# Local attention with a SiLU feed-forward gate on one core: four chunks of the attention output are turned by DMA on planes in the used-up tile of x, not by TensorE

## The chip, the core and the metric

The kernel runs on one core of a Trainium2 chip. The metric is the device time of one execution in microseconds (us); smaller is better. PE is TensorE (matmuls and transposes; PEld is its weight loading), DVE is VectorE, ACT is ScalarE, POOL is GpSimd, SP is SyncE, which in this kernel only issues transfers.

## The reference

Batch 1, S = 2048 tokens, D = 640, F = 1536, 32 heads of 20. All inputs and the output are float32.

```python
def _A_ref(x, wqkv, wo):                    # W, dil = 8, 2
    qkv = (x @ wqkv).reshape(B, S, 3, H, Dh).transpose(2, 0, 3, 1, 4)
    q, k, v = qkv[0], qkv[1], qkv[2]
    off = jnp.arange(W) * dil
    idx = jnp.arange(S)[:, None] - off[None, :]
    mask = idx >= 0
    ...
    logits = jnp.einsum("bhsd,bhswd->bhsw", q, kg) * Dh ** -0.5
    logits = jnp.where(mask[None, None, :, :], logits, -1e9)
    o = jnp.einsum("bhsw,bhswd->bhsd", softmax(logits), vg)
    return o.transpose(0, 2, 1, 3).reshape(B, S, D) @ wo

def _B_ref(x, w1, w2):
    return silu(x @ w1) @ w2

xn = layernorm(x)
out = x + _A_ref(xn, wqkv, wo) * silu(_B_ref(xn, w1, w2))
```

Each token looks at itself and the seven tokens 2, 4, ... 14 places before it.

## The kernel before, in words

**Tokens.** The 2048 tokens are worked in four groups, g = 0 to 3, of 512: two halves of the sequence, in each the even and the odd tokens. A group is four tiles t of 128 tokens. D = 640 is five chunks c of 128.

**Exact products.** A float32 matrix is kept as a high and a low part (fp32r), and a product is three matmuls: high by high, low by high, high by low. The turned x of a group stands in TH and TL (`th`, `tl` in rows), 128 columns of D on the partitions.

**Stages.** For each group `qkv_phase` computes q, k and v in four quarters of 160 columns (NQ = 4, CQ = 160; matmuls L960 to L962) and copies them out (ACT, L715 and L717); `halo` fetches the keys and values of neighbouring tokens (L728, L738 and L740 on SP). Attention runs on DVE with some help of POOL, quarter by quarter, and ends in the tile O (`o`; L754 and L757 are the scores, L774 is the exp, L796 to L809 the values). It lags behind PE and goes on during `ffn_phase`. There, twelve units of w1 (L1140 to L1142) and twelve of w2 (L1005, L1007) give the gate, evacuated with SiLU by ACT (L1224) into G (`gate`). Behind the first unit of w1 stands `wo_phase` of the group before, five chunks of wo, which needs the O of that group turned. `wo_last` does it for the last group.

**Turning O.** wo_phase reads O chunk by chunk with columns on the partitions, in OH and OL, which share memory with the TH and TL that the current group doesn't use. PE turns a chunk with `o_chunk`: four transposes of 128x128 into a PSUM bank `rot` (L629), a high part by ACT (L633), a low part by DVE (L639). This stands in the qkv phase of the next group, at the quarters and chunks of `O_AT`. Some chunks are turned by DMA (`turn_o`): `send` copies the chunk into two planes of 2-byte halves (ACT, L657), two DMA transposes turn them (SP, L662), and `join` puts the halves together (ACT, L670), then takes the high part (ACT, L676) and the low part (DVE, L677). `turn_x` does the same for chunks of the next group's x. The planes are borrowed memory: KV tiles for `turn_os`, the gate tile and the tile TURN for x. `O_DMA` names the chunks of O turned so: 0 and 1 of the second group (g=1), 0, 1 and 2 of the last.

**x.** XIN (`xin`) holds the x of the next group: loaded by SP (L600) at the start of ffn_phase, with statistics and normalisation on DVE (L607, L609, L615, L619) and a square root on ACT (L613), then turned. From then on it lies unused until the next load of x, or, at the end, until wo_last loads x again for the residual (L1085).

**Weights.** Seven ring slots (RING = 7, `w`). A unit is first loaded raw (SP, L538, into `xr` among others) and split by ACT (L574) and DVE (L578). Then it is either written to DRAM as both halves (`half_...`, SP, L583) or read again from there by POOL (L565) each time it is due. A transfer into a slot waits until PE has read the unit that stood there and, where that was written out, until that is done. The wo of the group g=2 is split anew and written out, with its loads at the end of that group's qkv.

**Order.** All work is first collected in a planner (`Weave`): each operation has an engine, an estimated length, the keys it reads and writes, a priority and an earliest time `at`. PE keeps the order in which the code adds its work; on the other engines the planner picks by estimated ready time and priority. What comes out is one fixed list for each engine; an engine runs its list in that order and waits where something isn't ready. `clock[0]` is the sum of PE's estimated work so far. `free_for(old, new)` hands memory from one set of names to another.

Of the kernel before, what the change touches and what calls it, by code (L numbers as in the profile page):

```python
# [8 lines left out]
F32 = mybir.dt.float32  # L9
# [6 lines left out]
P = 128  # L16
# [7 lines left out]
T = 4  # L24
# [33 lines left out]
O_OUT = (), (35.0, 55.0), (35.0, 55.0), (10.0, 25.0, 40.0)  # L58
O_BACK = (), (80.0, 82.0), (80.0, 82.0), (40.0, 55.0, 60.0)
X_BY = {1: 2, 3: 0, 4: 1}  # L60
SLOW, ISSUE, SUB_LATE = 8, 2.0, 3
PACE0, PACE = -20.0, 12.0
BACK = {1: 0.0, 2: 40.0}
QAT = 48
OAT = 16
STORE_Q = 1, 3
SHARED = (1, 0), (1, 2), (2, 0), (2, 2), (3, 0)
X_AT = 1.2, 6, 8
# [255 lines left out]
def local_attention_silu_ffn(ctx: ExitStack, tc: tile.TileContext, x, wqkv, wo, w1, w2, out):  # L324
# [152 lines left out]
    def store_at(u):  # L477

        return 1 + (u[0] == "wo" or u[0] == "q" and u[2] in STORE_Q)


    for u in units:
        n = seen[u] = seen.get(u, 0) + 1
        at = store_at(u)
        what.append("load" if n > at else "store" if n == at and n < again[u] else "split")
    fresh = [i for i, k in enumerate(what) if k != "load"]
# [13 lines left out]
    def raw_tile(k):  # L500
# [7 lines left out]
        return "xr", k % 3  # L508

    def raw_load(k):  # L510
# [12 lines left out]
        pairs = []  # L523
        if u[0] == "q":
            _, q, c = u
            whole = wqkv[c * P:(c + 1) * P, :]
            pairs.append((r.rearrange("p (k m) -> p k m", k=3), whole.rearrange("p (k m) -> p k m", k=3)[:, :, q * CQ:(q + 1) * CQ]))
        elif u[0] == "w1":
            pairs.append((r.rearrange("p (c f) -> p c f", c=DC),
                          w1.rearrange("(c p) f -> p c f", p=P)[:, :, u[1] * P:(u[1] + 1) * P]))  # L530
        else:
            m = wo if u[0] == "wo" else w2
            pairs.append((r, m[u[1] * P:(u[1] + 1) * P, :]))
        by = nc.scalar if k in BY_ACT else nc.sync

        def go():
            for to, frm in pairs:
                by.dma_start(to, frm)  # L538
# [3 lines left out]
        dma(go, [], kr, n * P * 4, 1 + k if k < 2 * DC else clock[0] + 5, (0.62 if k < 2 * DC else 0.45) * len(pairs))  # L542

    def raws_due(i, k):

        while rawn[0] < len(fresh) and fresh[rawn[0]] <= i + RAW_AHEAD and raw_in.get(raw_tile(rawn[0]), -1) <= k:
            raw_load(rawn[0])
            rawn[0] += 1

    def w_load():  # L550
# [10 lines left out]
        kh, kl = ("wh", s), ("wl", s)  # L561
        due = clock[0]
        if what[i] == "load":
            src = halves[u]
            add("POOL", 1.0, lambda: nc.gpsimd.dma_start(both, src), [("half", u)], [kh, kl], due + 10,  # L565
                nbytes=2 * n * P * 4)
            raws_due(i, sum(j < i for j in fresh) - 1)
            return
# [11 lines left out]
        if what[i] == "store":  # L580
            kept = dram.tile([P, 2, n], F32, name="half_" + "_".join(map(str, u)))
            halves[u] = kept
            dma(lambda: nc.sync.dma_start(kept, both.bitcast(F32)), [kh, kl], [("half", u)], 2 * n * P * 4, due + 25)  # L583
        raws_due(i, k)
# [60 lines left out]
    def both(k):  # L645
        return [k + (0,), k + (1,)]
# [33 lines left out]
    def turn_x(c, i, by, to, at, back):  # L680
# [3 lines left out]
             (chunk_span("x", c, True), chunk_span("x", c)))  # L684

    def turn_o(c, i, by, to, at, back):
# [494 lines left out]
    def ffn_phase(g, i, ix, io):  # L1181
# [12 lines left out]
        by_dma = X_DMA.get(g, ())  # L1194
        bufs = [("buf", c, h) for c in range(DC) for h in range(2)]
        for kind, f in plan(g):
            if kind == "w1":
                up(g, i, f, io)
            elif kind == "wo":
# [8 lines left out]
                for k, c in enumerate(by_dma):  # L1208
                    by = (piece(G, X_BY[c]), ("buf", X_BY[c])) if c in X_BY else (TURN, ("turn",))
                    turn_x(c, ix, by, (piece(G, c), ("buf", c)), clock[0] + PACE0 + PACE * k, clock[0] + BACK[g])  # L1210
            elif kind == "x":
# [13 lines left out]
        if g < NG - 1:  # L1225
            turn_os(g, i, begun)

    add("POOL", 0.7, consts, [], ["consts"], 0)
# [38 lines left out]
```

## Time and profile before

| what | value |
| --- | --- |
| median of 3 runs | 598.78 us (598.73 to 599.15) |
| profiled execution | 598.41 us |
| its span in the trace | 596.3 us |
| granted TensorE clock | 0.999 |
| busy: PE, DVE, ACT, POOL | 590.6, 513.3, 248.7, 168.2 us |

The span runs from the first to the last instruction in the trace; the 2.1 us between it and the execution's time lie around it. Busy times are of one execution. Rows in the trace give start, duration, engine, line and operation, with the idle time ahead of it and what ended it in brackets. A queue (SPq) row is an issue of a transfer, not its landing.

### The profile page before, as it was taken

The page shows a single profiled execution, that of the slowest core. Times are in us where ns is not written, and L with a number is a line of the kernel's source. Part 1 is how long each engine was busy: PE and PEld are TensorE (multiplying, and loading weights), DVE is VectorE, ACT ScalarE, POOL GpSimd, SP SyncE. Part 2 cuts the span into 40 slices and gives each one's busy share as a digit, 9 for nine tenths or more (in the row PEclk, how much of TensorE's full clock was granted, in tenths as well). Part 3 has the DMA queues.
Part 4 walks back from the last instruction along what each step waited for, and adds up shares of the span by engine and source line. Part 5 has one row for each costly group of instructions (what it writes and reads, how often), then busy time and mean ns, then how long its engine had stood idle before and what let it go on. Part 6 is the DMA issues. An engine that isn't in the chain of part 4 may idle for free.

```text
span 596.3 us, 9080 instructions
## 1 busy us (share of the span) xinstructions
PE 590.6 (99%) x3443; PEld 555.9 (93%) x3443; DVE 513.3 (86%) x505; ACT 248.7 (42%) x444; POOL 168.2 (28%) x229
## 2 busy tenths in 40 slices
PE   8999999999999999999999999999999999999997
PEld 7999999999999999999999999999999999999997
DVE  6499999999799978999988996999838799998744
ACT  5437375452545223747523604443412333335230
POOL 5800102233110153442221126543121233434100
PEclk9999999999999999999999999999999999999999
DMA  9999999879999999999699999998689999797952
GB/s 295 311 295 334 296 411 402 322 252 300 271 316 326 313 257 324 239 202 239 191 319 306 303 346 304 263 208 286 211 220 283 294 320 295 227 203 215 241 185 89
DMA packets 80263, 164.21 MB, mean 275 GB/s; under 512 B 19949, under 2 KB 44237, under 8 KB 80221
## 3 DMA queue, kind: packets, MB, share of 16 engines
q1 hardware_dynamic: 60381, 83.93, 52.1%
q0 software_dynamic: 19296, 79.31, 46.5%
q8 instruction: 27, 0.44, 0.3%
q10 hardware_dynamic: 544, 0.41, 0.2%
q14 instruction: 15, 0.12, 0.1%
HBM read 107.91 MB, written 34.16 MB: 238 GB/s over the span
## 4 chain that ended last, share of the span: by engine, by line
PE 98%; DMA 0%; DVE 0%; issue 0%
PE acc L1005 23%; PE acc L1007 15%; PE acc L960 10%; PE acc L961 10%; PE acc L962 10%; PE rot L1140 9%; PE rot L1142 9%; PE rot L1141 9%; PE acc L910 2%; PE rot L629 1%; DMA xin<-in_A_x_dram 0%; PE rot L894 0%; PE rot L1123 0%; DVE st L879 0%; PE rot L853 0%; DVE gate L1091 0%
## 5 line engine op out<-in xcount | busy, mean ns | idle before, releaser
L960 PE MATMUL acc<-w,th 128*128 128x480 f32 x300 | 110.6, 369 | 0.0
L961 PE MATMUL acc<-w,tl 128*128 128x480 f32 x300 | 109.8, 366 | 0.0
L962 PE MATMUL acc<-w,th 128*128 128x480 f32 x300 | 109.8, 366 | 0.0
L1005 PE MATMUL acc<-w,sh 128*128 128x384 f32 x384 | 108.6, 328 | 0.0
L1007 PE MATMUL acc<-w,sh 128*128 128x256 f32 x384 | 104.7, 273 | 0.0
L754 DVE TENSOR_TENSOR pr<-q,kv 128x2560 f32<-128x2560 f32 x32 | 90.2, 2819 | 15.9 <-DMA kv<-carry 12.7
L796 DVE TENSOR_TENSOR pr<-q,kv 128x2560 f32<-128x2560 f32 x32 | 91.5, 2860 | 1.4 <-DVE l L757 0.5
L1140 PE MATMUL rot<-th,w 128*128 128x512 f32 x240 | 91.8, 383 | 0.0
L1141 PE MATMUL rot<-tl,w 128*128 128x512 f32 x240 | 91.0, 379 | 0.0
L1142 PE MATMUL rot<-th,w 128*128 128x512 f32 x240 | 91.0, 379 | 0.0
L757 DVE TENSOR_REDUCE l<-pr 128x128 f32<-128x2560 f32 x32 | 89.7, 2804 | 0.2
L1153 ACT ACTIVATE sh<-rot 128x512 fp32r<-128x512 f32 x48 | 28.8, 599 | 134.2 <-PE rot L1142 134.1
L565 POOL DMA_DIRECT2D w<-half_w x72 | 39.0, 542 | 156.6 <-PE acc L1007 57.6
L1007 PEld LDWEIGHTS acc<-w,sh 128*128 128x128 f32 x384 | 73.7, 192 | 0.6
L1005 PEld LDWEIGHTS acc<-w,sh 128*128 128x128 f32 x384 | 72.6, 189 | 0.6
L565 POOL DMA_DIRECT2D w<-half_q x52 | 28.0, 538 | 119.8 <-PE acc L962 74.3
L962 PEld LDWEIGHTS acc<-w,th 128*128 128x128 f32 x300 | 56.7, 189 | 4.0
L960 PEld LDWEIGHTS acc<-w,th 128*128 128x128 f32 x300 | 56.7, 189 | 3.9
L961 PEld LDWEIGHTS acc<-w,tl 128*128 128x128 f32 x300 | 56.7, 189 | 3.9
L1005 PE MATMUL acc<-w,sl 128*128 128x384 f32 x192 | 55.9, 328 | 0.0
L1155 DVE TENSOR_TENSOR sl<-sf,sh 128x512 fp32r<-128x512 f32 x48 | 39.3, 819 | 16.8 <-ACT sf L1154 16.8
L1007 PE MATMUL acc<-w,sl 128*128 128x256 f32 x192 | 52.3, 273 | 0.0
(110 smaller groups left out, 1070.0 us busy)
## 6 DMA issues: line engine op xcount, KB each, us to landing
w<-half_w POOLq DMA_DIRECT2D x72, 640.0 KB, 7.0
w<-half_q POOLq DMA_DIRECT2D x52, 480.0 KB, 5.8
half_w<-w SPq DMA_DIRECT2D x24, 640.0 KB
half_q<-w SPq DMA_DIRECT2D x20, 480.0 KB
kv<-kv SPq DMA_DIRECT2D x15, 560.0 KB
w<-half_wo POOLq DMA_DIRECT2D x10, 640.0 KB, 5.6
kv<-kv SPq DMA_DIRECT2D x15, 420.0 KB
gate<-in_B_w_dram SPq DMA_DIRECT2D x16, 320.0 KB
```

Of the source, the lines that this page charges most:

```text
L565: add("POOL", 1.0, lambda: nc.gpsimd.dma_start(both, src), [("half", u)], [kh, kl], due + 10, nbytes=2 * n * P * 4)
L754: dve(2560, lambda: nc.vector.tensor_tensor(out=PR, in0=win(qq[:, t:t + 2, :], W, 0), in1=win(kv[:, 0, t:t + 2, :], W, CQ), op=OP.mult), h ...
L757: dve(2560, lambda: nc.vector.tensor_reduce(out=l[:, t:t + 2].rearrange("p t w h -> p (t w h)"), in_=PR.rearrange("p t w (h d) -> p (t w h ...
L796: dve(2560, lambda: nc.vector.tensor_tensor(out=PR.rearrange("p t w (h d) -> p t (w h) d", d=DH), in0=e[:, t:t + 2].rearrange("p t w h -> ...
L960: nc.tensor.matmul(o, hi, vh, start=c == 0, stop=False)
L961: nc.tensor.matmul(o, lo, vh, start=False, stop=False)
L962: nc.tensor.matmul(o, hi, vl, start=False, stop=c == DC - 1)
L1005: nc.tensor.matmul(a[t][0][:, :CA].rearrange("p (m h) -> p m h", h=2), st, col_a(w), start=first, stop=last)
L1007: nc.tensor.matmul(b[t // 2][0][:, h * CB:(h + 1) * CB].rearrange("p (m h) -> p m h", h=2), st, col_b(w), start=first and h == 0, stop=las ...
L1140: nc.tensor.matmul(to, wh[:, cs], hi, start=c == 0, stop=False)
L1141: nc.tensor.matmul(to, wh[:, cs], lo, start=False, stop=False)
L1142: nc.tensor.matmul(to, wl[:, cs], hi, start=False, stop=c == DC - 1)
```

## The change

A new table, `O_HOME`, names four more chunks of O that are turned by DMA: chunk 2 of g=1 and chunks 0, 1 and 2 of g=2. `qkv_phase` leaves them out on PE. The new `turn_home` adds them at the end of the group's own `ffn_phase`, behind `turn_os`: a chunk takes two pieces of XIN as its two planes, and the third chunk the last piece and TURN. `at` is given relative to the end of that ffn_phase, and `join` 20 us later. XIN is handed over ahead and back behind, so that the next load into it waits until the planes are read.

```diff
+O_HOME = {1: {2: 5.0}, 2: {0: -9.0, 1: -6.0, 2: -3.0}}
+HOME_BACK = 20.0
...
+    def turn_home(g, i):
+
+        todo = O_HOME.get(g, {})
+        if not todo:
+            return
+        old = [("xin", t) for t in range(T)]
+        place = [(piece(XIN, k), ("xp", k)) for k in range(DC)] + [(TURN, ("turn",))]
+        new = [k for _, p in place[:DC] for k in both(p)]
+        free_for(old, new)
+        for n, (c, at) in enumerate(todo.items()):
+            turn_o(c, i, place[2 * n], place[2 * n + 1], clock[0] + at, clock[0] + at + HOME_BACK)
+        free_for(new, old)
...
                         for k in O_AT.get((q, c), ()):
-                            if k not in O_DMA.get(g - 1, ()):
+                            if k not in O_DMA.get(g - 1, ()) and k not in O_HOME.get(g - 1, ()):
                                 o_chunk(g - 1, k, io)
...
         if g < NG - 1:
             turn_os(g, i, begun)
+            turn_home(g, i)
```

The rest of the diff adds settings that are empty or repeat the old values (`turn_first`, `STORE_W2`, `RAW_AGAIN`, `PACE0` as a table) and moves code into functions. It adds no instruction. Line numbers rise by 7 to 37: of what is spoken of here, L538 is now L545, L565 is L581, L574 is L590, L578 is L594, L583 is L577, L600 is L614, L607 is L621, L609 is L623, L619 is L633, L629 is L643, L633 is L647, L639 is L653, L657 is L671, L662 is L676, L670 is L684, L676 is L690, L677 is L691, L774 is L808, L1085 is L1119, L1153 to L1155 are L1187 to L1189, L1224 is L1261.

The lists move at three places that matter here.

SP at the end of the third group's qkv, before. `kv_96` is the last quarter's tile, `carry` the rows kept for the other half, `xr` takes raw weights (and x for the residual), `w_77` to `w_79` are ring slots with the first three chunks of wo:

```order
L738 DMA kv_96<-carry_121 1x2x640
L538 DMA xr_107<-in_A_wo_dram 128x640
L740 DMA kv_96<-carry_121 2x2x480
L538 DMA xr_108<-in_A_wo_dram 128x640
L583 DMA half_wo_167<-w_77 128x1280
L583 DMA half_wo_168<-w_78 128x1280
L583 DMA half_wo_169<-w_79 128x1280
L1053 DMA xr_109<-in_A_x_dram 128x640
```

The same place after the change, with the four loads of x around the raw loads of wo:

```order
L774 DMA kv_96<-carry_121 2x2x480
L614 DMA xin<-in_A_x_dram 128x640
L545 DMA xr_107<-in_A_wo_dram 128x640
L545 DMA xr_108<-in_A_wo_dram 128x640
L614 DMA xin<-in_A_x_dram 128x640 x3
L577 DMA half_wo_167<-w_77 128x1280
L577 DMA half_wo_168<-w_78 128x1280
L577 DMA half_wo_169<-w_79 128x1280
L1087 DMA xr_109<-in_A_x_dram 128x640
```

Before, the four loads stand some 12 rows ahead of this, behind the carry of the second quarter. Now they stand behind the carry of the last, and ahead of the stores of wo.

DVE at the start of the third group's FFN, before. L1155 is the low part of the first SiLU unit, `w_80` and `w_81` are the last two chunks of wo, which PE reads next; L780 to L783 and L796 belong to the attention:

```order
L780 TENSOR_REDUCE z_91<-q_97 128x32
L782 RECIPROCAL z_91<-z_91 128x32
L783 TENSOR_TENSOR q_97<-q_97,z_91 128x4x64
L1155 TENSOR_TENSOR sl_87<-sf,sh_84 128x512
L578 TENSOR_TENSOR w_80<-xr_107,w_80 128x640
L578 TENSOR_TENSOR w_81<-xr_108,w_81 128x640
L796 TENSOR_TENSOR pr<-q_97,kv_93 128x2560
```

The same place after:

```order
L653 TENSOR_TENSOR tl_74<-rot_120,th_70 128x512
L621 BN_STATS st_72<-xin 128x6 x2
L623 BN_AGGR mv<-st_72 128x2
L621 BN_STATS st_69<-xin 128x6 x2
L623 BN_AGGR mv<-st_69 128x2
L621 BN_STATS st_72<-xin 128x6 x2
L623 BN_AGGR mv<-st_72 128x2
L594 TENSOR_TENSOR w_80<-xr_107,w_80 128x640
L1189 TENSOR_TENSOR sl_87<-sf,sh_84 128x512
L594 TENSOR_TENSOR w_81<-xr_108,w_81 128x640
L629 RECIPROCAL sd<-sd 128x4
L633 TENSOR_SCALAR xin<-xin,mv,sd 128x640 x4
```

The statistics of x stood some 20 rows ahead of the two L578; those of the last three tiles now come right before the first L594, and the normalisation (L633) behind the second.

ACT at the end of the third group's FFN, before. `sf` is the last SiLU unit, L774 the exp of the last quarter's first half, L1224 frees the banks `acc` for the next qkv:

```order
L1154 ACTIVATE sf<-rot_119 128x512
L774 ACT_TABLE_LOAD
L774 ACTIVATE q_100<-l_104 128x4x64
L1224 ACT_TABLE_LOAD
L1224 ACTIVATE gate<-acc_113 128x2x192
L1224 ACTIVATE gate<-acc_114 128x2x192
L1224 ACTIVATE gate<-acc_117 128x4x128
```

The same place after, with the three copies of O into planes:

```order
L1188 ACTIVATE sf<-rot_120 128x512
L671 ACTIVATE xin<-o 128x1024 x3
L808 ACT_TABLE_LOAD
L808 ACTIVATE q_100<-l_104 128x4x64
L1261 ACT_TABLE_LOAD
L1261 ACTIVATE gate<-acc_113 128x2x192
L1261 ACTIVATE gate<-acc_114 128x2x192
L1261 ACTIVATE gate<-acc_117 128x4x128
L1261 ACTIVATE gate<-acc_115 128x2x192
```

The copies stand ahead of the exp and of the gate's evacuation. On PE the list only loses the sixteen transposes, four behind each of four matmuls; nothing else of it moves. On SP six DMA transposes come behind those of x and ahead of the fourth group's carry loads, two behind the first halos of the third group, and the six loads of L1085 go from behind the x transposes to behind the halos of the fourth group's second quarter.

More of the change, by code (lines that the diff above doesn't have):

```diff
@@ L484, in local_attention_silu_ffn @@
         at = store_at(u)
-        what.append("load" if n > at else "store" if n == at and n < again[u] else "split")
+        what.append("load" if n > at and u[1:] not in RAW_AGAIN.get((u[0], n), ()) else "store" if n == at and n < again[u] else "split")
     fresh = [i for i, k in enumerate(what) if k != "load"]
@@ L562, in w_load, with keep @@
         due = clock[0]
+        def keep():
+            kept = dram.tile([P, 2, n], F32, name="half_" + "_".join(map(str, u)))
+            halves[u] = kept
+            dma(lambda: nc.sync.dma_start(kept, both.bitcast(F32)), [kh, kl], [("half", u)], 2 * n * P * 4, due + 25)
         if what[i] == "load":
@@ L580, in w_load @@
         if what[i] == "store":
-            kept = dram.tile([P, 2, n], F32, name="half_" + "_".join(map(str, u)))
-            halves[u] = kept
-            dma(lambda: nc.sync.dma_start(kept, both.bitcast(F32)), [kh, kl], [("half", u)], 2 * n * P * 4, due + 25)
+            keep()
         raws_due(i, k)
@@ L1194, in ffn_phase @@
         by_dma = X_DMA.get(g, ())
-        bufs = [("buf", c, h) for c in range(DC) for h in range(2)]
+        bufs = [("buf", c, h) for c in range(DC) for h in range(2)] if g else []
+        if not g:
+            for k, c in enumerate(by_dma):
+                turn_first(c, ix, begun + X0_OUT + X0_PACE * k, begun + X0_BACK + X0_PACE * k)
         for kind, f in plan(g):
```

40 lines of the change are left out of this document (25 added, 15 removed).

## The prediction

> **What bounds the kernel.** I read the page first: busy shares and the chain that ended last.
>
> ```profile
> span 596.3 us, 9080 instructions
> PE 590.6 (99%) x3443; PEld 555.9 (93%) x3443; DVE 513.3 (86%) x505; ACT 248.7 (42%) x444; POOL 168.2 (28%) x229
> PE 98%; DMA 0%; DVE 0%; issue 0%
> ```
>
> TensorE (PE) is busy 99% of the span and carries 98% of the chain. Then its waits (us in total, times, longest), and three stretches of the span (length, then busy time of PE, PEld, DVE, ACT and POOL with their instructions, the granted clock, the share of the DMA engines, GB/s):
>
> ```profile
> PE rot L866 <- POOL ident masks.py:199: 1.4, 1, 1.4
> PE rot L894 <- DVE xin L884: 0.5, 1, 0.5
> 0.00:91.00 91.00, 89.05 (x476) 81.86 (x477) 75.97 (x111) 48.76 (x101) 25.05 (x28) 1.00 1.03 325
> ...
> 400.00:470.00 70.00, 70.00 (x396) 66.02 (x396) 51.99 (x45) 24.80 (x50) 16.17 (x29) 1.00 0.92 258
> ...
> 500.00:596.00 96.00, 92.56 (x583) 87.90 (x581) 73.30 (x76) 29.52 (x44) 23.20 (x31) 1.00 0.76 193
> ```
>
> PE has two waits, 1.9 us, both at the start; it loses 3.4 us at the end; between them it waits for nothing, as in the stretch from 400 to 470 that the change touches, and the granted clock is 1.00. So time is gained only by taking work off PE, and lost as soon as PE must wait for anything.
>
> **What leaves PE.** Four chunks of four transposes. One chunk stands thus in PE's order of time (start, duration):
>
> ```profile
> 320.18 0.37 PE L962 MATMUL acc<-w,th 128*128 128x480 f32 x1
> 320.38 0.60 PE L629 MATMUL rot<-ident,o 128*128 128x128 f32 x4
> 320.73 0.45 PE L960 MATMUL acc<-w,th 128*128 128x480 f32 x1
> 321.02 0.37 PE L961 MATMUL acc<-w,tl 128*128 128x480 f32 x1
> ```
>
> Durations overlap, so starts count. From the matmul before the chunk (320.18) to the second one behind it (321.02) is 0.84 us; two matmuls at their pitch of 0.20 (320.18 to 320.38) are 0.40. The chunk costs PE 0.44 us. Bounds: 0.35 (320.38 to 320.73) and 0.60 (its busy time). Two stretches of one group's qkv check it, the first with three chunks on PE, the second with five:
>
> ```profile
> 283.92:333.20 49.28, 49.28 (x249) 45.96 (x248) 43.92 (x48) 18.92 (x43) 8.60 (x16) 1.00 1.00 272
> 429.50:479.65 50.15, 50.15 (x257) 46.74 (x256) 34.16 (x25) 13.72 (x37) 10.60 (x20) 1.00 0.99 258
> ```
>
> 50.15 - 49.28 = 0.87 for two, 0.435 each. I take 4 x 0.44 = 1.76 us (1.4 to 2.4). One of the four falls in qkv of the third group (g=2), three in qkv of the fourth (g=3).
>
> The Trainium skill speaks against the change: "VectorE: DVE Perf Modes", section "The three transpose paths", gives 390 ns for a 128x128 bf16 transpose on TensorE and 1309 ns for one by DMA. By its figure sixteen transposes would free an estimated 6.2 us of TensorE; the trace's pitch, 0.11 us each, decides, and by it the sum stays 1.76.
>
> **What the DMA way adds.** The instructions that one chunk takes, old way and new, from their groups (min/median/max ns):
>
> ```profile
> L633 ACT ACTIVATE th<-rot x20: 579/597/598, 76.5 to 480.5; 128x512 fp32r<-128x512 f32 x20
> L639 DVE TENSOR_TENSOR tl<-rot,th x13: 680/684/692, 160.2 to 481.6; 128x512 fp32r<-128x512 f32 x13
> L657 ACT ACTIVATE kv<-o x5: 1039/1057/1062, 244.5 to 547.2; 128x1024 uint16<-128x1024 uint16 x5
> L670 ACT ACTIVATE kv<-kv x5: 1364/1370/1373, 272.0 to 563.1; 128x1024 uint16<-128x1024 uint16 x5
> L676 ACT ACTIVATE th<-kv x5: 621/631/636, 274.8 to 566.4; 128x512 fp32r<-128x512 f32 x5
> L677 DVE TENSOR_TENSOR tl<-kv,th x5: 674/682/687, 279.2 to 569.5; 128x512 fp32r<-128x512 f32 x5
> L662 SPq DMA_TRANSPOSE kv<-kv x10: 1189/1266/1571, 245.8 to 549.5; - x10
> ```
>
> ScalarE (ACT): 1.06 + 1.37 + 0.63 = 3.06 us a chunk for 0.60, so +9.8 us in four. ACT is at 24.8 of 70 us in the stretch from 400, so that is cover, except at one place (first rival). VectorE (DVE): 0.68 for 0.68, nothing. SyncE's queue (SP): eight transposes at 1.27, some 10 us of issue. Six stand ahead of the halo copies of the fourth group, two behind the first halos of the third. SP at the six:
>
> ```profile
> 408.20 8.79 SPq L1085 DMA_DIRECT2D xin<-in_A_x_dram  x6
> ...
> 417.73 0.42 SPq L740 DMA_DIRECT2D kv<-carry  x1
> 442.31 3.00 SPq L728 DMA_DIRECT2D kv<-kv  x4
> ```
>
> Behind 418.2 SP waits 24 us for its next work; six transposes need 7.6 and start at about 423 to 425. The halos at 442.31 aren't delayed. The six residual loads of L1085 leave 408 and go behind the halos of the second quarter of the fourth group. Only the last product reads them, more than 90 us later. Nothing on PE; bound above: their 8.8 us of issue hold up the next halos, which would delay DVE, not PE.
>
> **The moved loads of x.** The four loads of the fourth group's x (L600) leave 302.4 on SP and stand behind the third group's last carry, around the two raw loads of wo (L538) and ahead of the stores of half_wo. The reason: XIN serves as planes until then. Before:
>
> ```profile
> 302.41 3.03 SPq L600 DMA_DIRECT2D xin<-in_A_x_dram  x4
> ...
> 328.86 0.34 SPq L538 DMA_DIRECT2D xr<-in_A_wo_dram  x1
> ...
> 331.20 2.08 SPq L583 DMA_DIRECT2D half_wo<-w  x3
> ```
>
> and on DVE the first reader of the last of the four loads:
>
> ```profile
> 317.17 0.89 DVE L607 BATCH_NORM_STATS2 st<-xin 128x6 f32<-128x320 f32 x2 [1.18 <-DMA xin<-in_A_x_dram]
> ```
>
> The loads are 4 x 128 x 640 x 4 bytes = 1.31 MB. The next stretch is loaded already (last three columns: clock, share of the DMA engines, GB/s):
>
> ```profile
> 334.00:360.00 26.00, 26.00 (x166) 24.80 (x165) 24.30 (x22) 7.53 (x12) 5.66 (x9) 1.00 1.05 317
> ```
>
> At 317 GB/s the loads push what is behind them by up to 1.31/0.317 = 4.1 us, by nothing if they fill gaps. Behind them: the stores of half_wo, then the loads into the ring slots that those free (L565; first the POOL row, then the time to landing of that load), read by the fourth and fifth units of w1 (L1140):
>
> ```profile
> 360.04 0.53 POOL L565 DMA_DIRECT2D w<-half_w  x1 [1.79 <-DMA half_wo<-w]
> ...
> DMA to landing us min/median/max: 4.6/4.6/4.6
> ```
>
> and on PE the first matmuls of those units:
>
> ```profile
> 370.31 0.38 PE L1140 MATMUL rot<-th,w 128*128 128x512 f32 x1
> 373.55 0.38 PE L1140 MATMUL rot<-th,w 128*128 128x512 f32 x1
> ```
>
> The load of 360.04 waits for a store and lands 4.6 us later, at 364.6; the unit it feeds starts at 373.55. Less 0.44 (PE is earlier) that is 8.5 us of margin. The fifth unit's load now stands ahead of the fourth's, and the first residual product of L1054 ahead of both: 0.53 + 1.56 = 2.1 us. Against 4.1 + 2.1 some 2.3 us remain, so I put the cost at nothing.
>
> **Sum.** 598.41 (profiled execution, its span 596.3 and 2.1 outside) - 1.76 = 596.65. The median of the runs shown, 598.78, lies 0.37 above that execution: 598.78 - 1.76 = 597.02, so 597.0. The 1.9 and 3.4 us at the two ends stay.
>
> **Rivals.** *The last plane holds ACT (gain cancelled in part).* The copies of O into planes now stand on ACT ahead of an exp, a table load and the gate's SiLU (L1224), which frees the banks for the first matmul of the fourth group's qkv (the rows of DVE, ACT and PE in turn):
>
> ```profile
> 422.41 0.49 DVE L809 TENSOR_TENSOR o<-pr 128x320 f32<-128x320 f32 x1
> ...
> 423.92 0.42 ACT L774 ACTIVATE q<-l 128x256 f32<-128x256 f32 x1 [1.71 <-DVE l L772]
> 427.12 0.49 ACT L1224 ACTIVATE gate<-acc 128x384 f32<-128x384 f32 x1 [1.48 <-PE acc L1005]
> 429.50 0.37 PE L960 MATMUL acc<-w,th 128*128 128x480 f32 x1
> ```
>
> O's last piece ends at 422.90; third copy to 423.96, exp 0.42 with a table load on each side (423.92 to 427.12 less the 1.48 of waiting holds the exp and one load, 1.72, so 1.3 each): gate at about 427.0. The first bank is needed at 429.5 - 0.44 = 429.06 and takes 0.49, so ACT has 1.5 us left. Decides when O's piece is over 1.5 us later than now; at 2.9 later 1.4 us are lost and 598.4 results. Chance 0.08.
>
> *Weights late.* If the pushes on the POOL path add up to 8.5 us instead of 6.2, PE waits at the fourth or fifth unit of w1; 1.5 us more would leave 598.5. A page of the Trainium skill, "DMA: Bandwidth & Descriptors", section "Issuing engines are not separate DMA queues", says that transfers from all issuing engines run and interleave on the same 16 engines; by that the moved 1.31 MB also slow the other queue's loads. The 317 GB/s with a busy share of 1.05 agree that there is little room. Chance 0.12.
>
> *x lands late (slower).* On DVE the statistics of the fourth group's x (L607) now stand ahead of the low parts (L578) of the last two chunks of wo:
>
> ```profile
> 339.99 1.55 DVE L578 TENSOR_TENSOR w<-xr,w 128x640 fp32r<-128x640 f32 x2
> ```
>
> and PE's first wo matmul, and the first behind wo:
>
> ```profile
> 337.08 0.33 PE L1005 MATMUL acc<-w,th 128*128 128x384 f32 x1
> 353.53 0.38 PE L1140 MATMUL rot<-th,w 128*128 128x512 f32 x1
> ```
>
> Five chunks of wo take PE 353.53 - 337.08 = 16.45 us, 3.29 each: the fourth is needed at 346.95, now 346.5. Behind the last x come its statistics (0.89 + 0.2) and one L578 (0.78), 1.9 us, so it must land by 344.6. Issue: about 331, where the stores stood. Before, the last of the four, issued at about 305.1, landed at 317.17, 12 us later: 343, in time by 1.6 us. If it takes 17, PE waits 348 + 1.9 - 346.5 = 3.4 us: 598.78 - 1.76 + 3.4 = 600.4. It turns the sign at a landing of 346.4. For it: the stretch is full. Against it: the x loads are ahead of the stores and halos, not behind. Chance 0.14.
>
> **The numbers.** Forecast 0.66. Its range is 598.78 less 2.4 to less 1.4 us: 596.4 to 597.4. The first two rivals reach 598.5; the third leads up to 600.4. I end the range at 600.0, half-way into the third, and leave out under 0.1 there and some 0.05 below. A difference of 0.2%, 1.2 us, is about what a measurement tells from none: faster is below 597.6, slower above 600.0. Faster 0.66, same 0.20 (both first rivals), slower 0.14.
>
> **What would show it.** Right: PE's groups lose 16 transposes of O, its waits still list only the two at the start, qkv of the third and fourth groups take 0.44 and 1.3 us less, ACT's busy time rises by some 10 us. Wrong: a wait of PE on L578's w near 347 (x late), on L565's transfer near 370 to 374 (weights late), or on the gate of L1224 near 429 (last plane late). It would also be wrong if the stretch between the two qkv (about 333 to 429), which keeps its work, became longer.

## The result, and the profile after

The change made the kernel slower. Its median was 606.68 us (601.86, 602.57, 610.80 and 620.75) against 598.75 (598.63 to 599.15) on the same chip: 1.01 times, 95% interval 1.0062 to 1.0137. This ratio and those below leave out executions more than 1.5% above the fastest of the same kernel (here 620.75), so they say less than the median of a kernel that spreads. The forecast was 597.0. The profiled execution took 601.86 us, 2.5 of it outside its span; the other executions spread wider and upwards, which the four executions of before did not.

The head of the page after (span, busy time of each engine, shares of the chain that ended last) and the waits of PE (us in total, times, longest):

```profile
span 599.4 us, 9073 instructions
PE 590.1 (98%) x3427; PEld 555.3 (93%) x3427; DVE 515.2 (86%) x505; ACT 258.6 (43%) x452; POOL 164.5 (27%) x229
PE 92%; DVE 4%; DMA 2%; issue 1%; SPq 1%; ACT 0%; DVEq 0%
...
PE rot L1174 <- DVE tl L653: 4.0, 2, 2.1
PE rot L900 <- POOL ident masks.py:199: 1.4, 1, 1.4
PE rot L928 <- DVE xin L918: 0.3, 1, 0.3
```

PE has sixteen matmul instructions less, ACT 9.9 us more, as worked out. New is the first wait: twice, 4.0 us in all, PE waits ahead of a w1 unit for a low part of O (L653). The stretches of PE, before (first fence) and after (second): each from the last matmul of a group's qkv to the first of w1, from there to the next qkv, and after also the two qkv, whose rows of before stand in the prediction (length, busy time of PE, PEld, DVE, ACT, POOL, clock, DMA share, GB/s):

```profile
333.20:333.76 0.56, 0.56 (x6) 0.49 (x5) 0.56 (x1) 0.43 (x2) 0.00 (x0) 1.00 1.03 407
333.76:429.50 95.74, 95.74 (x600) 90.91 (x599) 87.88 (x72) 39.42 (x57) 36.12 (x48) 1.00 1.04 278
...
479.65:480.21 0.56, 0.56 (x6) 0.49 (x5) 0.56 (x1) 0.56 (x3) 0.00 (x0) 1.00 1.16 406
```

```profile
284.32:333.16 48.84, 48.84 (x245) 45.57 (x244) 40.57 (x34) 19.30 (x43) 8.59 (x16) 1.00 1.00 248
333.16:335.83 2.67, 0.80 (x6) 0.50 (x5) 2.67 (x3) 2.60 (x7) 0.53 (x1) 1.00 0.93 299
335.83:431.58 95.75, 95.75 (x596) 90.92 (x597) 89.98 (x83) 42.49 (x58) 35.33 (x47) 1.00 1.08 279
431.58:480.42 48.84, 48.84 (x245) 45.57 (x244) 35.19 (x25) 17.77 (x40) 10.60 (x20) 1.00 1.03 287
480.42:483.31 2.89, 0.81 (x6) 0.50 (x4) 2.89 (x3) 1.64 (x5) 0.49 (x2) 1.00 1.27 319
```

The two qkv are 0.44 and 1.31 us shorter, 1.75 together. Between last matmul of qkv and first of w1 lie 2.67 and 2.89 us where 0.56 was: 2.11 and 2.33 lost. With 0.39 from the start of the program, -1.75 + 2.11 + 2.33 + 0.39 = 3.1 us, the difference of the spans.

PE uses two banks `rot` in turn. The last two chunks of O are turned into them late in qkv, and the first w1 unit of the FFN takes the one of the fourth chunk, so it waits until DVE has made that chunk's low part. DVE before, in order of time, around the third group's:

```profile
327.39 2.81 DVE L757 TENSOR_REDUCE l<-pr 128x128 f32<-128x2560 f32 x1
330.12 0.68 DVE L639 TENSOR_TENSOR tl<-rot,th 128x512 fp32r<-128x512 f32 x1
330.72 0.61 DVE L770 TENSOR_REDUCE m<-l 128x32 f32<-128x256 f32 x1
331.37 0.43 DVE L772 TENSOR_TENSOR l<-l,m 128x256 f32<-128x256 f32 x1
331.71 2.82 DVE L754 TENSOR_TENSOR pr<-q,kv 128x2560 f32<-128x2560 f32 x1
```

After:

```profile
320.06 0.43 DVE L806 TENSOR_TENSOR l<-l,m 128x256 f32<-128x256 f32 x1
325.62 2.83 DVE L788 TENSOR_TENSOR pr<-q,kv 128x2560 f32<-128x2560 f32 x1 [5.14 <-DMA kv<-kv]
...
332.36 2.81 DVE L791 TENSOR_REDUCE l<-pr 128x128 f32<-128x2560 f32 x1
335.09 0.68 DVE L653 TENSOR_TENSOR tl<-rot,th 128x512 fp32r<-128x512 f32 x1
```

Before, the low part was through at 330.80, ahead of the score product of the second quarter (L754 at 331.71). Now that product (L788) and what hangs on it stand ahead of the low part in DVE's list. The statistics of x, on DVE from 312.89 to 318.30 before, had moved behind, and by the order of the rows the planner gave the free time to the product. But on the chip the product waits for halos: DVE stands idle 5.14 us with the rest of its list behind it. The Trainium skill, "PSUM — Partial Sum Buffer", section "Engine vs sequencer instructions", calls the queues of ScalarE, VectorE and GpSimd strict FIFO; the trace agrees, with those 5.14 us. At the fourth group, where it started at 476.78, the low part fell behind two more instructions (before, then after):

```profile
476.78 0.68 DVE L639 TENSOR_TENSOR tl<-rot,th 128x512 fp32r<-128x512 f32 x1
```

```profile
478.30 1.49 DVE L836 TENSOR_TENSOR kv<-pr 128x1280 f32<-128x1280 f32 x1
479.83 2.83 DVE L788 TENSOR_TENSOR pr<-q,kv 128x2560 f32<-128x2560 f32 x1
482.57 0.68 DVE L653 TENSOR_TENSOR tl<-rot,th 128x512 fp32r<-128x512 f32 x1
```

So much for 601.86. Two questions stayed: is the place in DVE's list the cause, and why do other executions of the same program take 606 to 620?

### The profile page after: what moved, and what is told of

Same layout as the page of the kernel before. It is cut to its first block, busy times and chain, and to the rows that moved or that the text cites. A ratio compares the mean times of both kernels' runs of the same rounds, so it can differ in the third digit from the quotient of the medians.

```text
span 599.4 us, 9073 instructions
## 1 busy us (share of the span) xinstructions
PE 590.1 (98%) x3427; PEld 555.3 (93%) x3427; DVE 515.2 (86%) x505; ACT 258.6 (43%) x452; POOL 164.5 (27%) x229
## 4 chain that ended last, share of the span: by engine, by line
PE 92%; DVE 4%; DMA 2%; issue 1%; SPq 1%; ACT 0%; DVEq 0%
PE acc L1039 22%; PE acc L1041 15%; PE rot L1174 9%; PE rot L1175 9%; PE rot L1176 9%; PE acc L996 8%; PE acc L994 8%; PE acc L995 8%; PE acc L944 2%; DMA kv<-kv 1%; DVE pr L788 1%; DVE l L791 1%; PE rot L643 1%; SPq L762 1%; DMA xin<-in_A_x_dram 1%
## 5 line engine op out<-in xcount | busy, mean ns | idle before, releaser
L788 DVE TENSOR_TENSOR pr<-q,kv 128x2560 f32<-128x2560 f32 x32 | 91.7, 2864 | 15.8 <-DMA kv<-kv 15.4
L581 POOL DMA_DIRECT2D w<-half_w x72 | 39.1, 543 | 160.5 <-PE acc L1041 60.3
L1187 ACT ACTIVATE sh<-rot 128x512 fp32r<-128x512 f32 x48 | 28.8, 599 | 125.1 <-PE rot L1176 125.1
L581 POOL DMA_DIRECT2D w<-half_q x52 | 28.0, 538 | 118.1 <-PE acc L996 73.4
L1174 PEld LDWEIGHTS rot<-th,w 128*128 128x128 f32 x240 | 45.4, 189 | 10.2 <-DVE tl L653 4.4
```

The source lines that it names most:

```text
L788: dve(2560, lambda: nc.vector.tensor_tensor(out=PR, in0=win(qq[:, t:t + 2, :], W, 0), in1=win(kv[:, 0, t:t + 2, :], W, CQ), op=OP.mult), h ...
L1174: nc.tensor.matmul(to, wh[:, cs], hi, start=c == 0, stop=False)
```

## Experiments

Fifteen kernels in four jobs. Times are us: median (lowest to highest, number of executions), the median of the kernel before in the same job, and the ratio with its 95% interval.

| kernel | time | before | ratio |
| --- | --- | --- | --- |
| a1_again | 606.63 (598.93 to 613.06, 12) | 598.80 | 1.0076 [1.0037, 1.0116] |
| a2_low_first | 599.34 (597.65 to 606.61, 12) | 598.80 | 1.0021 [0.9990, 1.0051] |
| a3_turn_soon | 600.38 (597.65 to 609.66, 12) | 598.80 | 1.0005 [0.9976, 1.0033] |
| a4_before_low_late | 600.88 (600.48 to 602.50, 11) | 598.80 | 1.0027 [1.0009, 1.0046] |
| b1_residual_last | 606.77 (598.61 to 621.44, 12) | 598.74 | 1.0058 [1.0023, 1.0093] |
| b2_low_first_residual_last | 599.33 (597.95 to 607.87, 12) | 598.74 | 1.0021 [0.9994, 1.0048] |
| b3_before_residual_late | 598.61 (597.99 to 599.77, 11) | 598.74 | 0.9994 [0.9985, 1.0002] |
| b4_all_three | 599.93 (596.79 to 611.83, 12) | 598.74 | 1.0018 [0.9983, 1.0053] |
| c1_low_ahead_of_halo | 598.77 (597.07 to 605.39, 12) | 598.71 | 1.0010 [0.9982, 1.0037] |
| c2_second_group_only | 606.00 (603.24 to 612.21, 6) | 598.71 | 1.0122 [1.0077, 1.0166] |
| c3_third_group_only | 601.77 (599.02 to 605.41, 12) | 598.71 | 1.0045 [1.0022, 1.0068] |
| c4_before_low_very_late | 611.93 (610.93 to 624.49, 4) | 598.71 | 1.0206 [1.0178, 1.0234] |
| d1_copies_for_transposes | 600.64 (599.29 to 604.36, 12) | 598.90 | 1.0012 [0.9986, 1.0038] |
| d2_third_group_mended | 598.31 (596.83 to 600.36, 12) | 598.90 | 0.9980 [0.9958, 1.0002] |
| d3_copies_and_mended | 597.39 (596.91 to 599.67, 12) | 598.90 | 0.9970 [0.9948, 0.9991] |

The kernel before has high executions too: 14 of its 122 in these jobs exceed 602 us, two of these, in the job of b1 to b4, exceed 1000. So a single high execution shows nothing; how many there are, and the median, do. Of twelve, 8 exceed 602 in a1, 5 in c3, 3 in d1, 2 in c1 and none in d2 and d3; of the six in c2, all do.

### The place of the low part

**a1_again**: the changed kernel as it is, once more.

> The changed kernel unaltered, for the size of the loss and its spread. Bank theory (the first w1 unit of the third and the fourth group's FFN waits for the PSUM bank that the low part of O's fourth chunk, L653 on DVE, frees late): the two waits of PE on L653 appear again, 2.1 and 2.3 us, and executions lie at 601.5 to 602.5, some of them higher. Rival (DMA traffic of the moved x loads): waits elsewhere, different from run to run.

Its best executions are level with before, its worst 14 us above; none lies at the expected 601.5 to 602.5. The profiled one took 599.33 and had one of the two waits (2.2 us, in the fourth group). A single profile of this kernel doesn't tell its time.

**a2_low_first**: the low part of the fourth chunk one place earlier in DVE's list, in both groups (`pinned` holds the two).

```diff
+        for p in self.pinned:
+            at = done.index(p)
+            q = max(k for k in range(at) if done[k].eng == "DVE" and done[k].dur > 0)
...
+            done.insert(at, done.pop(q))
```

> The changed kernel, and in the finished list of DVE two neighbours exchanged at two places: the low part of O's fourth chunk stands one instruction earlier, ahead of the score reduction (third group) and ahead of the score product (fourth group). Nothing else moves. Bank theory: both waits of PE go (the low part ends at about 333.1 and 480.5, the first w1 unit is due at 333.7 and 481.0), 4.4 us come back and the 1.76 us off PE are seen: 597.0, and the spread goes too. Rival (DMA traffic, or the copies on ACT): the time stays at 601 to 602.

PE's one wait behind the start in its profiled execution (599.32):

```profile
PE acc L1050 <- DVE gate L1083: 0.8, 2, 0.6
```

The wait for the low part is gone, and the median falls 7.3 us. A smaller one is new: w2 waits for the gate's product (L1083), which frees its banks. Before, it stood directly behind the value product and started at 500.84; here one more score product is ahead of it and it starts at 505.00. Some executions still reach 606.61, so this is not all.

**a3_turn_soon**: PE turns the last two chunks of O earlier.

```diff
-                        for k in O_AT.get((q, c), ()):
+                        for k in (O_AT if g - 1 not in O_HOME else O_SOON).get((q, c), ()):
...
+    O_SOON = {(2, 4): (3,), (3, 2): (4,)}
```

> The changed kernel, and the two chunks of O that PE still turns in the third and fourth group's qkv stand earlier: the fourth chunk behind the last chunk of the third quarter, the fifth behind the third chunk of the last quarter. The planner orders DVE anew. Bank theory: the fourth chunk's low part is done 5 us or more ahead of the first w1 unit, no wait of PE in the middle: 597.0. Rival: 601 to 602 as before the edit.

No wait for a low part in its profile, waits for the gate's product as in a2 (1.4 us), and the same spread, up to 609.66.

**a4_before_low_late**: the other way round, the kernel before with the low part put behind the next score product at both places (`nth` is 0).

```diff
+            q = [k for k in range(at, len(done)) if done[k].eng == "DVE" and done[k].dur > 2.5][self.nth]
...
+            done.insert(q, done.pop(at))
```

> The kernel before (nothing turned anew), and in the finished list of DVE only the low part of O's fourth chunk stands later at two places: behind the next score product. Bank theory: PE waits at the first w1 unit of the third and fourth group's FFN, about 1.5 us (low part done at 335.2 instead of 330.8, unit due at 333.76) and 2.1 us (482.3, due at 480.21): 602.3. Rival (DMA traffic): the transfers are untouched, 598.8.

```profile
PE rot L1151 <- DVE tl L648: 2.0, 2, 1.0
```

This order alone, without any DMA turn, gives the wait and costs about 2 us, in all eleven executions alike (602.3 was expected: the two waits are 0.9 and 1.0 us). The place of the low part is shown as a cause, from both sides. Alone it makes no spread.

### The spread

**b1_residual_last**: the six residual loads (L1119) behind the last halos, since as it stands they are ahead of some.

```diff
+        h = [done.index(o) for o in self.halos[3, 3]]
+        at = max(h) + 1
...
+        done[at:at] = self.res
```

> The changed kernel, with only the six loads of the residual x (L1119) moved on SP: from ahead of the third quarter's halos of the last group to behind those of its last quarter. Halo theory (those 1.31 MB delay the third quarter's halos from 481.6 to 487 to 490, close to DVE's need at about 491; in executions where they land later still, DVE is late with the product by the gate, L1074, and the low parts, and PE waits many us): the spread of 599 to 613 goes, the two bank waits of PE on L653 remain or the second shrinks: 599 to 601.5, none above 604. Rival (the spread comes from the x loads and stores near 330 to 360): still 606 and more in half the executions.

The spread is the widest of all. In its profile PE waits 4.7 us once, at the fourth group, and the clock falls; three stretches of 2 us there (columns as above):

```profile
480.00:482.00 2.00, 0.00 (x0) 0.00 (x0) 1.97 (x2) 0.29 (x2) 0.00 (x0) 1.00 1.32 356
482.00:484.00 2.00, 0.00 (x0) 0.00 (x0) 2.00 (x2) 0.00 (x0) 0.31 (x2) 0.52 1.16 340
...
486.00:488.00 2.00, 2.00 (x6) 1.58 (x5) 1.97 (x3) 0.00 (x0) 0.84 (x1) 0.50 1.05 222
```

The granted clock is 0.50 until about 488.9, and the first w1 unit takes 5.65 us from its first matmul to wo's first, instead of 3.34. The residual loads as a cause are refuted, and a long wait is seen to cost 2.3 us more than itself.

**b2_low_first_residual_last**: the edits of a2 and b1 together.

> Both edits: the low part of O's fourth chunk one place earlier on DVE at the two places, and the residual loads behind the last halos. Bank and halo theory together: no wait on L653, no spread; left is a wait of about 1.4 us on the product by the gate (L1074), which stands behind one more score product than before: 598.0 to 598.5, none above 600. Rival: median 599.3 with some at 605 to 607, as with the first edit alone.

The same as a2 within 0.01 us in the median, and five executions above 600, where none was expected: the rival's forecast.

**b3_before_residual_late**: the kernel before with those loads where the change puts them.

```diff
+        at = min(done.index(o) for o in self.halos[3, 2])
...
+        done[at:at] = self.res
```

> The kernel before, with only the six residual loads (L1085) moved on SP from 408 us to where the change puts them, ahead of the third quarter's halos of the last group. Nothing is turned anew. Halo theory: those halos land 5 to 8 us later, at 487 to 490 where DVE needs them at 491; a spread like that of the changed kernel appears, best executions at 598.8, several at 602 to 608. Rival (the spread belongs to the turning or to the x loads): 598.5 to 599.5 as before.

No cost: the interval of the ratio is 0.9985 to 1.0002.

**b4_all_three**: b2, and the gate's product again ahead of the score product.

```diff
+        at = min(done.index(o) for o in self.gates)
+        q = max(k for k in range(at) if done[k].eng == "DVE" and done[k].dur > 0)
...
+        k = done.index(last) + 1
+        done[k:k] = go
```

> The edits of the low part and of the residual loads, and on DVE the product by the gate of the third group (L1074, six instructions) ahead of the score product that the change put in front of it. Theory: no wait of PE is left behind the first 25 us, all of the 1.76 us off PE shows: 597.0, none above 599. Rival: another wait turns up, 598 to 599.

Its three best executions, 596.79, 596.80 and 597.24, are where the forecast was. But five are above 604, and the profiled one (604.66) has PE waiting 4.1 us for the third group's low part, since a product ahead of it waited for halos:

```profile
PE rot L1206 <- DVE tl L681: 4.1, 1, 4.1
...
331.95 2.83 DVE L816 TENSOR_TENSOR pr<-q,kv 128x2560 f32<-128x2560 f32 x1 [9.32 <-DMA kv<-kv]
```

The same product ran at 325.62 in the profile of the change: here the halos of the second quarter are some 6 us later. What is new ahead of them on SP are the two DMA transposes of the one chunk of the second group.

**c1_low_ahead_of_halo**: the third group's low part now ahead of that product, the fourth's two places earlier, and the gate's product first (`behind(q, p)` moves the instruction at place q, and what depends on it, behind p).

```diff
+            behind([k for k in before if done[k].dur > 2.5][-2] if n == 0 else before[-2], p)
```

> The changed kernel, and on DVE alone: in the third group the low part of O's fourth chunk stands ahead of the second quarter's score product, which waits for halos (before the edit it stood behind that and its reduction); in the fourth group it stands directly behind the value product (two places earlier); and the product by the gate stands ahead of the score product in front of it. Queue theory (the spread is the landing of the second quarter's halos, handed on to PE through DVE's order and the PSUM bank): the bank waits and most of the spread go: median 597.2, at most two executions above 601. Rival (the spread comes from anything else, such as weights or DMA transposes on another path): half of the executions stay above 599, as with the earlier edits of DVE.

The median equals before (597.2 was expected); three executions are above 601, where at most two were expected. The profiled one was the worst, and shows other waits of PE, three of them:

```profile
PE acc L1015 <- ACT xin L703: 1.5, 1, 1.5
PE acc L1060 <- DVE sl L1212: 1.4, 1, 1.4
...
PE rot L1197 <- DMA w<-half_w: 0.5, 1, 0.5
```

L703 is the `join` of the one chunk of the second group: it stands in ACT's list ahead of what frees banks, and waits for the transposes. In this execution the order on DVE didn't cure late transfers; over twelve it takes the median 7.9 us under a1's.

**c2_second_group_only** and **c3_third_group_only**: one chunk alone, or the other three.

```diff
-O_HOME = {1: {2: 5.0}, 2: {0: -9.0, 1: -6.0, 2: -3.0}}
+O_HOME = {1: {2: 5.0}}
```

```diff
-O_HOME = {1: {2: 5.0}, 2: {0: -9.0, 1: -6.0, 2: -3.0}}
+O_HOME = {2: {0: -9.0, 1: -6.0, 2: -3.0}}
```

> Only chunk 2 of the second group is turned by DMA (one of the four). The x loads are moved as in the change. Queue theory: the third group's stage is as in the changed kernel (bank wait of about 2 us, more where halos land late), the fourth group's as before: 0.44 us gained, 600 to 601 in good executions, a spread to 606 and more. Rival (each chunk brings its share): 598.4.

> Only chunks 0, 1 and 2 of the third group are turned by DMA (three of the four). The x loads stay at 302 us. Queue theory: no wait and no spread at the third group's FFN; at the fourth's the low part of the fourth chunk stands behind three more instructions, a wait of about 2 us, less the 1.32 off PE: 599.5, spread of 1 to 3 us. Rival (the DMA transposes themselves make the spread): 599 to 608 as with the whole change.

The one chunk alone costs 7.3 us (600 to 601 was expected), the three together 3.1 (599.5 was expected). Each price holds the changed place of a low part as well as the transposes. In c3's profile (604.40) PE waits 3.7 us once, for the fourth group's low part, and the clock falls behind it. In c2's (607.61) the wait is 7.3 us long, with this ahead of it on SP (the two transposes, then the next halos) and on DVE:

```profile
301.53 5.98 SPq L676 DMA_TRANSPOSE xin<-xin  x2
...
309.23 5.86 SPq L762 DMA_DIRECT2D kv<-kv  x4
...
331.10 2.82 DVE L788 TENSOR_TENSOR pr<-q,kv 128x2560 f32<-128x2560 f32 x1 [7.34 <-DMA kv<-kv]
```

In the profile of the change the same two transposes were issued in 3.35 us from 301.58, and the product ran at 325.62. Their packets in the records ran from 306.19 to 310.07 there, from 306.50 to 317.72 in c2, from 307.21 to 320.10 in c1: 3.9, 11.2 and 12.9 us for the same 0.26 MB. The other queue's loads in that stretch (300 to 318; number, size, median us to landing) are late with them. In the order the change, c2, c1 (before: 8.7):

```profile
w<-half_q POOLq DMA_DIRECT2D x7, 480.0 KB, 8.5
```

```profile
w<-half_q POOLq DMA_DIRECT2D x7, 480.0 KB, 12.7
```

```profile
w<-half_q POOLq DMA_DIRECT2D x8, 480.0 KB, 15.8
```

The profiled kernels without these two transposes (before, a4, b3, c3, c4, d1, d2, d3) gave 7.2 to 9.2; of the nine with them, six gave 7.4 to 8.7 and three 12.7 to 15.8 (b4 15.3). In these three all of the core's transfers are slow, not the transposes alone: from 306 to 318 us they moved 151 to 156 GB/s, in the other six 279 to 308, in those without 305 to 359. Their DMA share is no lower for it (1.32 to 1.40, in the change 1.33). The change, then c2 (columns as above):

```profile
306.00:318.00 12.00, 12.00 (x61) 11.20 (x60) 9.93 (x5) 4.46 (x10) 2.65 (x5) 1.00 1.33 290
```

```profile
306.00:318.00 12.00, 12.00 (x61) 11.21 (x60) 6.69 (x3) 2.45 (x8) 2.63 (x5) 1.00 1.32 156
```

**c4_before_low_very_late**: the kernel before with the low part behind that product and its reduction, to price a long wait without any DMA turn.

```diff
+            a, b = [o for o in done[at:] if o.eng == "DVE" and o.dur > 2.5][:2]
...
+            done.insert(done.index(b) + 1, p)
```

> The kernel before, and on DVE only the low part of O's fourth chunk is placed later still, behind the next score product and its reduction, in both groups. PE then waits 5.1 us (low part done at 338.8, unit due at 333.76) and about 5.3 us. Clock theory (an idle PE of some 4 us and more is granted half the clock for about 4 us after it starts again, some 2 us lost each time): 598.8 + 10.4 + 4.2 = 613.4, mean clock near 0.99. Rival (only the waits count): 609.2, clock 1.00.

```profile
PE rot L1155 <- DVE tl L652: 7.3, 2, 3.8
...
336.00:338.00 2.00, 0.42 (x1) 0.42 (x2) 2.00 (x3) 1.30 (x3) 0.00 (x0) 0.58 1.01 296
338.00:340.00 2.00, 2.00 (x6) 1.55 (x6) 1.43 (x4) 0.88 (x1) 0.00 (x0) 0.50 1.08 285
```

Waits of 3.5 and 3.8 us, and the two w1 units behind them take 6.08 and 6.26 us instead of 3.32: 13.0 us together, for a median 13.2 above before. The waits alone would have given 598.7 + 7.3 = 606.0; the clock's part, 5.7, is nearly as large as theirs.

### Both causes apart

**d1_copies_for_transposes**: plain copies of the same bytes in place of the eight new transposes.

```diff
-            dma(lambda h=h: nc.sync.dma_start_transpose(
+            dma(lambda h=h, off=len(mute): nc.sync.dma_start(
+                b.bitcast(U16).rearrange("p (h n) -> p h n", h=2)[:, h],
+                a.bitcast(U16).rearrange("p (h n) -> p h n", h=2)[:, h]) if off else nc.sync.dma_start_transpose(
```

> The changed kernel, with each of the eight new DMA transposes replaced by a plain DMA copy of the same 128 x 1024 bytes at the same place, so these four chunks of O are not turned (their share of the output is left out of the computation). Everything else, the order too, is as in the change. Transpose theory (the transposes' small packets, slow in full queues, hold up the halos behind them): the second quarter's halos land by 322 to 325 in the third group, the wait of PE on L653 there goes or is under 2 us, and the spread goes: 597.5 to 600, none above 602. Rival (the queues are full anyway): 599 to 613 as with the change.

The highest of twelve is 604.36 instead of 613.06, and the median 6.0 us under a1's (measured on another chip, where before's median is 0.1 higher). Weight loads as before, and a short wait for halos:

```profile
w<-half_q POOLq DMA_DIRECT2D x7, 480.0 KB, 8.1
...
323.45 2.83 DVE L794 TENSOR_TENSOR pr<-q,kv 128x2560 f32<-128x2560 f32 x1 [1.41 <-DMA kv<-kv]
```

Three executions exceed 602, where none was expected. The profiled one, the highest, has the fourth group's wait for the low part and one for ACT's gate, which the forecast's first rival named. And although the first of these lasts only 2.1 us, the clock falls behind it:

```profile
PE rot L1180 <- DVE tl L653: 2.1, 1, 2.1
PE acc L1000 <- ACT gate L1267: 2.1, 1, 2.1
...
485.50:486.00 0.50, 0.50 (x4) 0.38 (x3) 0.50 (x1) 0.00 (x0) 0.48 (x2) 0.56 1.14 378
...
488.50:489.00 0.50, 0.50 (x3) 0.38 (x2) 0.50 (x1) 0.00 (x0) 0.00 (x0) 0.52 1.05 255
489.00:489.50 0.50, 0.50 (x5) 0.47 (x4) 0.50 (x1) 0.11 (x1) 0.00 (x0) 1.00 1.14 241
```

PE starts again at 484.16; the clock is at half from about 485.5 to 489, and the unit takes 5.03 us, 1.3 more than the 3.34 and another wait of 0.4 explain.

**d2_third_group_mended**: the three chunks of c3, with the fourth group's low part two places earlier and the gate's product first.

```diff
-O_HOME = {1: {2: 5.0}, 2: {0: -9.0, 1: -6.0, 2: -3.0}}
+O_HOME = {2: {0: -9.0, 1: -6.0, 2: -3.0}}
...
+            behind(before[-2], p)
```

> Only chunks 0, 1 and 2 of the third group are turned by DMA, and on DVE the fourth chunk's low part stands directly behind the value product in the fourth group, the product by the gate ahead of the score product in front of it. Theory: 1.32 us off PE, the third group undisturbed, the low part no longer two instructions late: 597.4 to 598, some executions 1 to 3 us higher where the halos land late (the low part is still behind the score product that waits for them). Rival: 600 to 602 as without the two edits.

PE waits only at the start (its two rows are those of before). The best single execution is 596.83, and the median 0.6 us under before (597.4 to 598 was expected), at a ratio of 0.9980 whose interval ends at 1.0002: the only complete version with chunks turned anew whose median is under before's, but not clearly faster. It differs from c3 only in the two moves on DVE, and its median is 3.5 us lower.

**d3_copies_and_mended**: the copies of d1 with c1's order on DVE.

> The plain copies instead of the eight transposes (four chunks not turned), together with the mended order of DVE at the three places (low part ahead of the score product that waits for halos, or behind the value product; gate product first). If the two causes named are all, nothing is left but the 1.76 us off PE: 597.0, none above 599. Rival (a third cause): a spread above 600 remains.

The lowest median, in a narrow range: 596.91 to 599.67, 0.9948 to 0.9991 of before. One execution is above 599, where none was expected. With both causes taken away 1.5 of the 1.75 us that PE saves come out. It is no version to use, since a copy turns nothing.

Four of these kernels differ only in the two causes (medians in us; those of before in their jobs are 598.71 to 598.90):

| order on DVE | transposes | copies |
| --- | --- | --- |
| as in the change | 606.63 (a1) | 600.64 (d1) |
| mended | 598.77 (c1) | 597.39 (d3) |

Mending the order is worth 7.9 us beside the transposes and 3.3 beside the copies. Copies are worth 6.0 us with the order of the change, and 1.4 with the mended one, where the two intervals overlap. So the two causes work together: late halos cost most where the low part that PE needs stands behind the product that waits for them.

## Why the prediction was wrong, point by point

- **What leaves PE: right.** Said 1.76 us, 0.44 and 1.3 by stretch; measured 1.75, 0.44 and 1.31. The 6.2 us that the prediction worked out from the Trainium skill's figure would have been 3.5 times too much.
- **ACT: right.** Said +9.8 us beside PE's work, measured +9.9. The last plane did not hold the gate in the profile of the change; it did in d1's.
- **DVE, "0.68 for 0.68, nothing": the step that failed.** It counted DVE's time and left out its order. The low parts of the chunks that stay on PE free a bank that PE needs next, and their place in the list moved with the statistics of x. The working noted that move, but asked only what it does to L578. Price in the profiled execution 2.11 + 2.33 us, more than the saving. Shown by a2 (taken away) and a4 (put in alone); with all three places mended and the transposes kept, 7.9 us less (c1 against a1).
- **SP, "eight transposes at 1.27" of issue: the second failure.** It counted issue and not landing, and of the two in the third group it said only that they stand behind the first halos. They stand ahead of the next ones. In some executions they take 11 to 13 us instead of 4, and halos and weights behind them are late. Shown by d1 (copies: 6.0 us less than a1) and the rows of c2, whose 7.3 us for one chunk hold the place of the low part too. With the order mended the transposes cost 1.4 us (c1 against d3), not clear of noise.
- **A wait was priced at its length.** Those of 3.5 us and more brought PE's clock to 0.50 and cost 1.6 to 2.9 us more; of four of about 2 us one did (d1, 1.3 us; why, stands below). In c2, 7.3 us of wait and a first unit of 4.93 instead of 3.32 us make 8.9 of the 9.5 by which its span exceeds before's.
- **x loads and residual loads at nothing: right as transfers.** The stretch from w1 to the next qkv is 95.75 us against 95.74, so neither x nor the weights were late in the profile of the change; b3 shows the residual loads. But the moved loads of x took the statistics along, and with them the order on DVE: c3, which leaves them and that group's chunk as before, has before's order in the third group.
- **Rivals.** The sign was the third's, the mechanism none of the three. The mark "longer between the two qkv" did show: 98.42 us (333.16 to 431.58) against 96.30.

Open: why the same two transposes take 4 us in one execution and 11 to 13 in another, with all of the core's transfers at half their rate; and, as the executions of the change at 606 to 621 have no trace, what share of each is late transfers, waits and clock. That they are of the kinds traced in b1, b4, c2 and d1 is likely, not shown.

## What to carry to other kernels

On an in-order engine, ask of every edit what now stands ahead of the instruction that frees a PSUM bank, and whether that waits for a transfer: a cost of 0 us of busy time can be 4 us of PE. A transfer added to a full queue is priced by its landing and by what lands behind it, over several executions. PE's own saving must be compared with the longest wait it may cause, and that wait can cost 1 to 3 us beyond its length through the clock.

## What the hardware showed that I had not expected

**The clock.** All six waits of PE of 3.5 to 7.3 us that I traced (two in c4, one each in b1, b4, c2, c3) took the granted clock to 0.50, and the next w1 unit took 4.93 to 6.26 us instead of about 3.3. Waits of 1.87, 2.1 (the change) and 2.2 us (a1) left it at 1.00, one of 2.07 us (d1) did not. The Trainium skill, "TensorE: Matmul & The Clock Gate", section "Part 1: The HAM clock gate (the "warmup" mystery)", states half the clock after an idle window of about 3.4 us, full clock after a busy one of about that length, and a window that runs freely. The runs agree with the window: the clock stays at 0.50 for 3.41 us (b4, c3, d1) or 6.83 (b1, c2, both times in c4), and the two starts in c4 lie 153.6 us apart, 45 times 3.413. They differ on the idle time. I counted steps of 3.413 us from each trace's first rise of the clock. Each step in which PE ran no matmul for 2.01 us or more was followed by 0.50; none at full clock with 1.80 us or less was. In d1 2.01 of the 2.07 us fall into one step, while the waits of the change are split (1.19 and 0.68, 1.39 and 0.70), and so is a1's (0.45 and 1.80). So in these traces what a wait of 2 us costs depends on where it falls, which is luck.

**The transposes.** Seven of twelve executions of the change (a1) took longer than the longest of twelve with copies of the same bytes (606.58 us and more against 604.36). The Trainium skill's "Advanced Engine Details and Errata", section "X-Bar Transpose (TRN2)", calls transpose DMAs as fast as regular ones. In the profile of the change they are (packets from 306.19 to 310.07; those of the copies from 305.73 to 311.88 in d1 and 305.56 to 308.65 in d3); in c1 and c2 the packets run until 320.10 and 317.72.
